# Rows of softmax weights stored token-innermost, denominators per two token tiles, and buffers of one phase handed to the next tile by tile

## The chip, the cores and the metric

The kernel runs on one NeuronCore of one Trainium2 chip. The metric is the device time of one execution in microseconds (us), lower is better; the time given is the median of several runs. A profile is one further execution, recorded instruction by instruction. TensorE is called PE below (PEld: its weight loads), VectorE DVE, ScalarE ACT, GpSimd POOL, and SyncE SP. POOL and SP also issue the DMA transfers, each from a queue that is worked through in order.

## What is computed

The reference is an attention with 32 memory slots, followed by a mixture-of-depths feed-forward step.

```python
# B=8 batches, H=8 heads, S=576 tokens, head_dim=64, 32 memory slots; D=512, F=1024, capacity=128
a = exp(phi - max(phi, axis=2)); a = a / (sum(a, axis=2) + 1e-9)   # softmax over tokens
k_m = einsum('bhsm,bhsd->bhmd', a, k)
v_m = einsum('bhsm,bhsd->bhmd', a, v)
scores = q @ k_m.T / 8;  attn = softmax(scores over the 32 slots)
x = (attn @ v_m), heads side by side                               # (B, S, 512)
score = x @ w_gate
# per batch: the 128 tokens of highest score get x + sigmoid(score) * (relu(x @ w1) @ w2); the others keep x
```

## The kernel before, in words

The program is written in an explicit order: Python generators (`softmax`, `keys`, `split_v`, `values`, `centre`, `scores`, `attend`, `rank`, `gather`, `ffn`) emit instructions and hand over at each `yield`. `turns(jobs, lag, width)` lets several jobs take turns, a new one starting every `lag` rounds; `beside(main, other, n)` gives `other` n steps after each step of `main`. Every engine works through its own instructions in the order in which they were emitted. A tile pool with `bufs` buffers makes a new tile wait for the readers and writers of the tile that had its memory.

There are four phases.

1. Softmax of batches 0 to 3, a group being one batch and four heads (so 8 groups). A group is a tile of 128 partitions (4 heads of 32 slots) by 576 tokens; `softmax` runs its long exact exponential on DVE and ACT and leaves the weights in tile `e` (last instruction L262). Beside it `split_v` (L271 to L279) splits the values into high and low parts and writes them to the DRAM scratch `vparts`.
2. Softmax of batches 4 to 7, and beside it `values(0)`.
3. Attention, ranking and feed-forward of batches 0 to 3, and beside it `values(1)`.
4. The same for batches 4 to 7, with nothing beside it.

After each group's softmax, `keys` (L287 on) turns the weights with six PE transposes (L293) into `aS` with the tokens on the partitions, copies them out with ACT (L295), and after a `yield` splits `aS` on DVE into a high part `ahi` (L299, a mask) and a low part `alo` (L301, a subtraction). POOL then writes both to the DRAM scratch `aparts` in eight DMAs (L305) and doubles them there with two DRAM-to-DRAM copies (L311). The keys' products `k_m` follow on PE (L315).

`values(st)` accumulates `v_m` for four batches exactly from the parts. It loads pieces of 32 tokens (T = 32, 18 pieces): `v_rows` with two DMAs on SP (L334) and `a_rows` with eight DMAs, four on SP and four on POOL (L340), into two buffers each. For each token it issues four matmuls (L353), one per batch, each on 32 rows of the array with a weight load of 128 columns from `a_rows` and 128 moving columns from `v_rows`: 2304 matmuls in each of phases 2 and 3. In `a_rows` the tile is laid out token, head pair, slot, so that the 128 weights of one token lie side by side. A step of the generator is 16 matmuls.

Between phases 2 and 3 the pools of the softmax (`io`, `ex`) are closed, and `work`, `one` and `step` are opened over the same memory. The order on SP there is: the feed-forward weights `w1_sb` (L695) and `w2_sb` (L696), the queries of batch 0 (`load_q`, L100), then the first `v_rows` and `a_rows` of `values(1)`.

`attend` computes for all five token tiles the denominators with ten small matmuls (L493, `heads_of` moving), turns them into reciprocals `rd` on DVE (L498, L500) and a count of good entries (L503), and then goes through the token tiles in pairs: the output products (L510, L512), the scaling by `rd` (L516), POOL's addition of the mean (L519), the score on DVE (L480 to L485) and the store (L523).

Of the kernel before, what the change touches and what calls it, by code (L numbers as in the profile page):

```python
# [18 lines left out]
PSUM = bass.MemoryType.PSUM  # L19

P = 128
NC = 6


# [14 lines left out]
def kernel(  # L39
# [25 lines left out]
    F = w1.shape[1]  # L65
    KD, KF = D // P, F // P
    SET = 4
    T = 32
    scale = 1.0 / Dh ** 0.5
    out_flat = out.rearrange("b s d -> (b s) d")  # L70

# [7 lines left out]
    accp = ctx.enter_context(tc.tile_pool(name="accp", bufs=1, space=PSUM))  # L79
    pss = ctx.enter_context(tc.tile_pool(name="pss", bufs=4, space=PSUM))  # L80
    first = ExitStack()
    io = first.enter_context(tc.tile_pool(name="io", bufs=2))
    ex = first.enter_context(tc.tile_pool(name="ex", bufs=2))

# [27 lines left out]


    v_rows = [rows.tile([P, 2, T, Dh], F32R, name=f"v_rows{i}") for i in range(2)]
    a_rows = [rows.tile([P, T, NPR, M], F32R, name=f"a_rows{i}") for i in range(2)]
    for t in v_rows + a_rows:
        nc.gpsimd.memset(t.bitcast(F32), 0.0)
    for t in kbd + vbd + vls:
# [6 lines left out]
    heads_of = const.tile([P, 4], F32, name="heads_of")  # L125
    ones3 = const.tile([3, P], BF16, name="ones3")
    ones = const.tile([P, 1], F32, name="ones")
    good = const.tile([P, B], F32, name="good")

    tgs = [const.tile([P, NT, 2], F32, name=f"tg{i}") for i in range(3)]  # L130

# [135 lines left out]
    def split_v(b):  # L267

        for u in range(2):
            vb = io.tile([P, S * Dh * NPR // P], F32, name="vb")  # L270
            nc.sync.dma_start(out=vb, in_=v[b, u])  # L271
            hi = io.tile([P, S * Dh * NPR // P], F32, name="vhi")
            nc.vector.tensor_single_scalar(hi.bitcast(I32), vb.bitcast(I32), -4096,
                                           op=ALU.bitwise_and)
            nc.vector.tensor_sub(vb, vb, hi)
            yield
            for vp, src in enumerate((vb, hi)):
                for ap in range(2):
                    nc.gpsimd.dma_start(  # L279
                        out=vparts[u, b, ap, vp].rearrange("r s d -> (r s d)")  # L280
                                                .rearrange("(p x) -> p x", p=P), in_=src)
            yield
# [3 lines left out]
    def keys(b, g):  # L286
        a = soft.pop((b, g))  # L287
        kb = ks.pop((b, g))
        aS = ex.tile([PT, NC, P], F32, name="aS")
        for c0 in range(0, NC, 3):  # L290
            tp = bank([PT, 3, P])
            for c in range(3):
                nc.tensor.transpose(out=tp[:, c], in_=a[:, (c0 + c) * PT:(c0 + c + 1) * PT],  # L293
                                    identity=ident)
            nc.scalar.activation(aS[:, c0:c0 + 3], tp, AF.Copy)  # L295
        yield
        hi = ex.tile([PT, NC, P], F32, name="ahi", bufs=1)
        lo = ex.tile([PT, NC, P], F32, name="alo", bufs=1)
        nc.vector.tensor_single_scalar(hi.bitcast(I32), aS.bitcast(I32), -4096,  # L299
                                       op=ALU.bitwise_and)  # L300
        nc.vector.tensor_sub(lo, aS, hi)  # L301
        for h in range(4):
            r, u = 2 * g + h // 2, h % 2
            for part, src in enumerate((lo, hi)):
                nc.gpsimd.dma_start(  # L305
                    out=aparts[r, u, b, part, 0].rearrange("(c p) m -> p c m", p=PT),
                    in_=src[:, :, h * M:(h + 1) * M])
        for part in range(2):
            copies = aparts[2 * g:2 * g + 2].rearrange("r u b t w s m -> b t w (r u) (s m)")[b, part]
            copies = copies.rearrange("w h (x y) -> w x h y", x=16)  # L310
            nc.gpsimd.dma_start(out=copies[1], in_=copies[0])  # L311
        km = bank([P, 2, 2 * M])
        for rr in range(2):
            for c in range(NC):
                nc.tensor.matmul(out=km[:, rr], lhsT=kb[:, c, rr * P:(rr + 1) * P],  # L315
                                 rhs=aS[:, c, rr * 2 * M:(rr + 1) * 2 * M],
                                 start=(c == 0), stop=(c == NC - 1))
        yield
        for u in range(2):
            part = slice(u * Dh, (u + 1) * Dh)  # L320
            nc.scalar.activation(kbd[b][part, 2 * g:2 * g + 2, u * M:(u + 1) * M],
                                 km[part, :, u * M:(u + 1) * M], AF.Copy)

    def values(st):

        accs = [accp.tile([P, 512], F32, name=f"acc{i}") for i in range(SET)]
        b0 = st * SET

        def load(ch):
            ss = slice(ch * T, (ch + 1) * T)
            for u in range(2):
                nc.sync.dma_start(  # L334
                    out=v_rows[ch % 2][u::2, u].rearrange("p s d -> p (s d)").bitcast(F32),
                    in_=vparts[u, b0:b0 + SET].rearrange("b t w r s d -> (b t w r) (s d)")
                        [:, ch * T * Dh:(ch + 1) * T * Dh])
            for r in range(NPR):
                for u in range(2):
                    (nc.sync, nc.gpsimd)[u].dma_start(  # L340
                        out=a_rows[ch % 2][2 * r + u::8, :, r].bitcast(F32),
                        in_=aparts[r, u, b0:b0 + SET].rearrange("b t w s m -> (b t w) s m")[:, ss])

        n = S // T
        load(0)
        for ch in range(n):
            if ch + 1 < n:
                load(ch + 1)
            vr, ar = v_rows[ch % 2], a_rows[ch % 2]
            for s in range(T):  # L350
                for bb in range(SET):
                    p = slice(bb * 32, bb * 32 + 32)
                    nc.tensor.matmul(out=accs[bb][:, :P].rearrange("p (u d) -> p u d", d=Dh),  # L353
                                     lhsT=ar[p, s].rearrange("p r m -> p (r m)"), rhs=vr[p, :, s],
                                     start=(ch == 0 and s == 0), stop=(ch == n - 1 and s == T - 1))
                if s % 4 == 3:
                    yield
        for bb in range(SET):
            v_m[b0 + bb] = const.tile([P, P], F32, name=f"v_m{b0 + bb}")
            nc.scalar.activation(v_m[b0 + bb], accs[bb][:, :P], AF.Copy)  # L360
# [126 lines left out]
    def attend(b, general):  # L487
        eT, tg = eTs[b % 2], tgs[b % 3]
        row, rest = mean[b]
        den = bank([P, NT, 2, 4])  # L490
        for c in range(NT):
            for g in range(2):
                nc.tensor.matmul(out=den[:, c, g], lhsT=eT[:, g, c * P:(c + 1) * P], rhs=heads_of,  # L493
                                 start=True, stop=True)
        yield
        rd = step.tile([P, NT, H], F32, name="rd")
        rd_f = rd.rearrange("p c h -> p (c h)")
        nc.vector.tensor_scalar(out=rd_f, in0=den.rearrange("p c g h -> p (c g h)"),  # L498
                                scalar1=float(M), scalar2=1e-9, op0=ALU.add, op1=ALU.add)
        nc.vector.reciprocal(rd_f, rd_f)  # L500
        if not general:
            ok = step.tile([P, NT * H], F32, name="ok")
            nc.vector.tensor_scalar(out=ok, in0=rd_f, scalar1=1e-30, scalar2=0.0, op0=ALU.is_gt,  # L503
                                    op1=ALU.add, accum_out=good[:, b:b + 1])
        for c0 in range(0, NT, 2):
            cols = min(2, NT - c0)
            x = step.tile([P, 2, D], F32, name="xj", bufs=3)[:, :cols]
            for c in range(cols):
                o = bank([P, D])
                nc.tensor.matmul(out=o, lhsT=ones3, rhs=rest, start=True, stop=False)  # L510
                for g in range(2):
# [3 lines left out]
                yield  # L515
                nc.vector.tensor_mul(x[:, c].rearrange("p (h d) -> p h d", d=Dh),  # L516
                                     o.rearrange("p (h d) -> p h d", d=Dh),
                                     rd[:, c0 + c].unsqueeze(2).to_broadcast([P, H, Dh]))
            nc.gpsimd.tensor_add(x, x, row.unsqueeze(1).to_broadcast([P, cols, D]))  # L519
            yield  # L520
            score(tg[:, c0:c0 + cols, 1], x, cols)
# [1 line left out]
            nc.gpsimd.dma_start(  # L523
                out=out[b, c0 * P:c0 * P + (cols - 1) * P + n].rearrange("(c p) d -> p c d", p=n),
                in_=x[:n])
        if len(tiles) and tiles[-1] < P:
            nc.gpsimd.memset(tg[tiles[-1]:, NT - 1, 1:2], 0.0)

    def rank(b):
# [102 lines left out]
            in_=ye[:n], in_offset=None)  # L632

    def attention_and_ffn(b, general=False):
        if not general:
            for j in range(2):
                load_q(b, j)
        yield from centre(b)
# [48 lines left out]
    finish(sums)  # L687
    first.close()

    work = ctx.enter_context(tc.tile_pool(name="work", bufs=3))  # L690
    one = ctx.enter_context(tc.tile_pool(name="one", bufs=1))
    step = ctx.enter_context(tc.tile_pool(name="step", bufs=2))
    w1_sb = one.tile([P, KD, F], F32, name="w1_sb")
    w2_sb = one.tile([P, KF, D], F32, name="w2_sb")
    nc.sync.dma_start(out=w1_sb, in_=w1.rearrange("(t p) f -> p t f", p=P))  # L695
    nc.sync.dma_start(out=w2_sb, in_=w2.rearrange("(t p) f -> p t f", p=P))  # L696

# [1 line left out]
    for t in eTs:  # L699
# [4 lines left out]
    finish(sums)  # L704
    finish(turns([attention_and_ffn(b) for b in range(SET, B)], 14, 3))

    ps = bank([1, B])
    nc.tensor.matmul(out=ps, lhsT=ones, rhs=good, start=True, stop=True)
    bad = work.tile([1, B], I32, name="bad")
    nc.vector.tensor_scalar(out=bad, in0=ps, scalar1=-1.0, scalar2=float(P * NT * H),  # L710
                            op0=ALU.mult, op1=ALU.add)
    any_bad = work.tile([1, 1], I32, name="any_bad")
    nc.vector.tensor_reduce(any_bad, bad, axis=AX.X, op=ALU.max)
# [37 lines left out]
```

## Time and profile before

| | |
|---|---|
| Median of 3 runs | 1171.39 us (1164.1 to 1179.52) |
| The profiled execution | 1177.25 us, of which the span of the recorded instructions is 1175.4 us |
| PE busy | 662.3 us, 56% |
| DVE busy | 765.7 us, 65% |
| ACT busy | 293.0 us, 25% |
| POOL busy | 351.3 us, 30% |
| DMA | 165.50 MB in 124930 packets, 84784 of them under 512 B |

The span is the time from the first to the last recorded instruction; the execution's own time is 1.85 us more. Shares of busy time are averages over the four phases, which have different limits, so what follows is read phase by phase. In a row of the timeline the columns are: start, duration, engine, line, operation, output and inputs, number of instructions merged, and in brackets the idle time before with what ended it. A matmul of f32 data that is not marked f32r is recorded as two.

### The profile page before, as it was taken

To read this page: it belongs to the slowest core of one execution; us is meant where nothing else is said; L and a number is where in the kernel's file an instruction comes from. 1 tells how busy PE (TensorE), PEld (TensorE's weight loads), DVE (VectorE), ACT (ScalarE), POOL (GpSimd) and SP (SyncE) were. 2 spreads that over 40 slices of the span, in tenths; PEclk is the share of its full clock that TensorE was granted. 3 is DMA by queue.
4 is the path that set the end of the run, shared out by engine and by line. 5 is a ranking of instruction groups with operands and counts; after the bars stand their busy time and mean duration, and the time that the engine had idled before them with its cause. 6 is when DMAs were issued, how large, how long until landed. Compare 5 with 4: busy or idle time off the path is not lost. (4 is left out here: it accounts for less than half of the span.)

```text
span 1175.4 us, 15823 instructions
## 1 busy us (share of the span) xinstructions
PE 662.3 (56%) x6138; PEld 492.3 (42%) x6138; DVE 765.7 (65%) x1283; ACT 293.0 (25%) x561; POOL 351.3 (30%) x529
## 2 busy tenths in 40 slices
PE   0020202222014777697621259999999977588866
PEld 0020202222014776687621237766766644345432
DVE  8777989999887998999988114343333314565450
ACT  2121312333323332233332010303012121331320
POOL 9133432221124434443212413233232401233230
PEclk9999999999999999999999999999577987598897
DMA  4898994211235979768621656666755712211110
GB/s 139 292 376 296 320 364 130 71 51 26 65 100 108 205 172 226 180 156 156 147 59 40 178 161 159 139 163 142 176 131 128 194 34 66 73 59 38 41 58 13
DMA packets 124930, 165.50 MB, mean 141 GB/s; under 512 B 84784, under 2 KB 95024, under 8 KB 120240
## 3 DMA queue, kind: packets, MB, share of 16 engines
q1 hardware_dynamic: 98352, 84.69, 30.0%
q0 software_dynamic: 26496, 79.72, 21.9%
q8 instruction: 51, 0.84, 0.3%
q14 instruction: 31, 0.25, 0.1%
HBM read 105.64 MB, written 68.16 MB: 148 GB/s over the span
## 5 line engine op out<-in xcount | busy, mean ns | idle before, releaser
L353 PE MATMUL acc<-v_rows,a_rows 32*128 32x128 f32 x4608 | 243.4, 378 | 86.9 <-DMA a_rows<-aparts 86.4
L353 PEld LDWEIGHTS acc<-v_rows,a_rows 32*128 32x128 f32 x4608 | 224.2, 288 | 139.7 <-issue 127.6
L293 PE MATMUL bank<-ident,e 128*96 128x128 f32 x96 | 23.9, 421 | 353.3 <-DVE e L262 353.3
L293 PEld LDWEIGHTS bank<-ident,e 128*96 128x96 f32 x96 | 16.7, 193 | 356.3 <-issue 306.6
L340 POOL DMA_DIRECT2D a_rows<-aparts x144 | 90.2, 633 | 180.2 <-PE acc L353 160.6
L305 POOL DMA_DIRECT2D aparts<-alo x64 | 47.5, 742 | 241.0 <-DVE alo L301 214.7
L315 PE MATMUL bank<-aS,kb 96*128 96x64 f32 x384 | 86.1, 423 | 11.7 <-ACT aS L295 11.7
L315 PEld LDWEIGHTS bank<-aS,kb 96*128 96x128 f32 x384 | 83.1, 331 | 16.6 <-ACT aS L295 15.9
L611 PE MATMUL bank<-w_sb,xeT 128*128 128x512 f32 x128 | 73.0, 709 | 3.4 <-ACT xeT L602 3.4
L519 POOL TENSOR_TENSOR xj<-xj,mean 128x1024 f32<-128x1024 f32 (+1 forms) x24 | 47.7, 1988 | 73.0 <-DVE xj L516 72.9
L512 PE MATMUL bank<-vbd,eT 128*128 128x256 f32 x160 | 66.4, 556 | 0.0
L516 DVE TENSOR_TENSOR xj<-bank,rd 128x512 f32<-128x512 f32 x40 | 27.6, 689 | 56.8 <-PE bank L512 56.6
L622 PE MATMUL bank<-w_sb,hT 128*128 128x512 f32 x128 | 62.3, 620 | 0.2 <-ACT hT L602 0.2
L168 ACT ACTIVATE vh<-num 128x576 int16<-128x576 f32 x32 | 21.8, 682 | 135.3 <-DVE num L212 135.3
L480 DVE TENSOR_TENSOR prod<-xj,wg 128x1024 f32<-128x1024 f32 (+1 forms) x24 | 25.1, 1046 | 46.6 <-POOL xj L519 46.6
L207 DVE SCALAR_TENSOR_TENSOR lo<-num,vh 128x576 f32<-128x576 f32 x48 | 36.2, 754 | 21.7 <-ACT vh L168 21.7
L211 DVE TENSOR_TENSOR low<-low,lo 128x576 f32<-128x576 f32 x64 | 48.5, 758 | 2.2
L305 POOL DMA_DIRECT2D aparts<-ahi x64 | 47.7, 745 | 2.1 <-DMA a_rows<-aparts 1.6
L209 DVE TENSOR_TENSOR lo<-lo,rh 128x576 f32<-128x576 f32 x64 | 48.0, 750 | 0.0
L512 PEld LDWEIGHTS bank<-vbd,eT 128*128 128x128 f32 x160 | 38.4, 265 | 18.7 <-issue 13.7
L556 DVE SCALAR_TENSOR_TENSOR cmp<-row,tg,wide 128x576 bf16<-128x576 f32 x40 | 32.7, 817 | 17.7 <-ACT row L542 16.8
L627 DVE SCALAR_TENSOR_TENSOR ye<-bank,gr,xe 128x512 f32<-128x512 f32 x8 | 6.0, 750 | 56.3 <-PE bank L622 56.3
(152 smaller groups left out, 1269.4 us busy)
## 6 DMA issues: line engine op xcount, KB each, us to landing
v_rows<-vparts SPq DMA_DIRECT2D x72, 512.0 KB, 5.9
vparts<-vb POOLq DMA_DIRECT2D x32, 576.0 KB, 5.9
vparts<-vhi POOLq DMA_DIRECT2D x32, 576.0 KB, 7.7
kb<-in_k SPq DMA_DIRECT2D x16, 576.0 KB, 7.7
vb<-in_v SPq DMA_DIRECT2D x16, 576.0 KB, 7.5
aparts<-aparts POOLq DMA_DIRECT2D x32, 288.0 KB, 3.2
a_rows<-aparts SPq DMA_DIRECT2D x144, 64.0 KB, 6.7
a_rows<-aparts POOLq DMA_DIRECT2D x144, 64.0 KB, 6.1
```

The lines of the kernel that those rows point to most:

```text
L207: stt(out=lo, in0=val, scalar=GRID, in1=h, op0=ALU.mult, op1=ALU.subtract)
L209: tt(out=lo, in0=lo, in1=rh, op=ALU.mult)
L211: tt(out=low, in0=low, in1=lo, op=ALU.add)
L293: nc.tensor.transpose(out=tp[:, c], in_=a[:, (c0 + c) * PT:(c0 + c + 1) * PT], identity=ident)
L305: nc.gpsimd.dma_start(out=aparts[r, u, b, part, 0].rearrange("(c p) m -> p c m", p=PT), in_=src[:, :, h * M:(h + 1) * M])
L315: nc.tensor.matmul(out=km[:, rr], lhsT=kb[:, c, rr * P:(rr + 1) * P], rhs=aS[:, c, rr * 2 * M:(rr + 1) * 2 * M], start=(c == 0), stop=(c = ...
L340: (nc.sync, nc.gpsimd)[u].dma_start(out=a_rows[ch % 2][2 * r + u::8, :, r].bitcast(F32), in_=aparts[r, u, b0:b0 + SET].rearrange("b t w s ...
L353: nc.tensor.matmul(out=accs[bb][:, :P].rearrange("p (u d) -> p u d", d=Dh), lhsT=ar[p, s].rearrange("p r m -> p (r m)"), rhs=vr[p, :, s], ...
L512: nc.tensor.matmul(out=o[:, g * 4 * Dh:(g + 1) * 4 * Dh], lhsT=eT[:, g, (c0 + c) * P:(c0 + c + 1) * P], rhs=vbd[b % 3][:, g], start=False, ...
L519: nc.gpsimd.tensor_add(x, x, row.unsqueeze(1).to_broadcast([P, cols, D]))
L611: nc.tensor.matmul(out=ps[:n], lhsT=xeT[:, d, :n], rhs=w1_sb[:, d, f0:f0 + 512], start=(d == 0), stop=(d == KD - 1))
L622: nc.tensor.matmul(out=ps[:n], lhsT=hT[:, f, :n], rhs=w2_sb[:, f], start=(f == 0), stop=(f == KF - 1))
```

## The change

- `aparts` is laid out in DRAM as 18 pieces of 32 slots by 32 tokens, token innermost. `a_rows` is laid out head pair, slot, token, so a piece's row is 4 KB in one run on both sides, and the weights of one token are read from `a_rows` with a step of 32 elements (128 B).
- The high and low parts are split from `e` itself (128 partitions by 576), ahead of the transposes and of the `yield`, and written to `aparts` from there.
- `vb` and `vhi` of `split_v` get a pool of their own, `vio`. The pools of phases 3 and 4 are opened with `reuse_waits="tile"`, in the order `work`, `weights`, `step`, `one`. The queries of batch 0 are loaded ahead of the feed-forward weights.
- `attend` computes denominators for each pair of token tiles inside the loop, with no `yield` of their own. The count of good entries becomes one comparison on the scores at the end (a score times zero must be zero).

```diff
+    vio = first.enter_context(tc.tile_pool(name="vio", bufs=2))
...
-    a_rows = [rows.tile([P, T, NPR, M], F32R, name=f"a_rows{i}") for i in range(2)]
+    a_rows = [rows.tile([P, NPR, M, T], F32R, name=f"a_rows{i}") for i in range(2)]
...
     def keys(b, g):
         a = soft.pop((b, g))
         kb = ks.pop((b, g))
+        hi = ex.tile([P, S], F32, name="ahi", bufs=1)
+        lo = ex.tile([P, S], F32, name="alo", bufs=1)
+        nc.vector.tensor_single_scalar(hi.bitcast(I32), a.bitcast(I32), -4096, op=ALU.bitwise_and)
+        nc.vector.tensor_sub(lo, a, hi)
+        for h in range(4):
+            r, u = 2 * g + h // 2, h % 2
+            for part, src in enumerate((lo, hi)):
+                nc.gpsimd.dma_start(
+                    out=aparts[r, u, b, part, 0].rearrange("c m s -> m c s"),
+                    in_=src[h * M:(h + 1) * M].rearrange("m (c s) -> m c s", s=T))
+        for part in range(2):
+            copies = aparts[2 * g:2 * g + 2].rearrange("r u b t w c m s -> b t w (r u) (c m s)")[b, part]
+            copies = copies.rearrange("w h (x y) -> w x h y", x=16)
+            nc.gpsimd.dma_start(out=copies[1], in_=copies[0])
         aS = ex.tile([PT, NC, P], F32, name="aS")
...
-        hi = ex.tile([PT, NC, P], F32, name="ahi", bufs=1)
-        lo = ex.tile([PT, NC, P], F32, name="alo", bufs=1)
-        nc.vector.tensor_single_scalar(hi.bitcast(I32), aS.bitcast(I32), -4096,
-                                       op=ALU.bitwise_and)
-        nc.vector.tensor_sub(lo, aS, hi)
...
                 (nc.sync, nc.gpsimd)[u].dma_start(
-                        out=a_rows[ch % 2][2 * r + u::8, :, r].bitcast(F32),
-                        in_=aparts[r, u, b0:b0 + SET].rearrange("b t w s m -> (b t w) s m")[:, ss])
+                        out=a_rows[ch % 2][2 * r + u::8, r].rearrange("p m s -> p (m s)").bitcast(F32),
+                        in_=aparts[r, u, b0:b0 + SET].rearrange("b t w c m s -> (b t w) c (m s)")[:, ch])
...
-                                     lhsT=ar[p, s].rearrange("p r m -> p (r m)"), rhs=vr[p, :, s],
+                                     lhsT=ar[p].rearrange("p r m s -> p (r m) s")[:, :, s], rhs=vr[p, :, s],
...
     def attend(b, general):
-        den = bank([P, NT, 2, 4])
-        for c in range(NT):
-            for g in range(2):
-                nc.tensor.matmul(out=den[:, c, g], lhsT=eT[:, g, c * P:(c + 1) * P], rhs=heads_of,
-                                 start=True, stop=True)
-        yield
-        rd = step.tile([P, NT, H], F32, name="rd")
...
         for c0 in range(0, NT, 2):
             cols = min(2, NT - c0)
+            den = bank([P, 2, 2, 4])[:, :cols]
+            for c in range(cols):
+                for g in range(2):
+                    nc.tensor.matmul(out=den[:, c, g], lhsT=eT[:, g, (c0 + c) * P:(c0 + c + 1) * P],
+                                     rhs=heads_of, start=True, stop=True)
+            rd = step.tile([P, 2, H], F32, name="rd")[:, :cols]
+            nc.vector.tensor_scalar(out=rd.rearrange("p c (g h) -> p c g h", g=2), in0=den,
+                                    scalar1=float(M), scalar2=1e-9, op0=ALU.add, op1=ALU.add)
+            nc.vector.reciprocal(rd, rd)
...
+        if not general:
+            nc.vector.tensor_scalar(out=good[:, b], in0=tg[:, :, 1], scalar1=0.0, scalar2=0.0,
+                                    op0=ALU.mult, op1=ALU.is_equal)
...
-    work = ctx.enter_context(tc.tile_pool(name="work", bufs=3))
-    one = ctx.enter_context(tc.tile_pool(name="one", bufs=1))
-    step = ctx.enter_context(tc.tile_pool(name="step", bufs=2))
-    w1_sb = one.tile([P, KD, F], F32, name="w1_sb")
-    w2_sb = one.tile([P, KF, D], F32, name="w2_sb")
+    work, weights, step, one = (
+        ctx.enter_context(tc.tile_pool(name=name, bufs=bufs, reuse_waits="tile"))
+        for name, bufs in (("work", 3), ("weights", 1), ("step", 2), ("one", 1)))
+    for j in range(2):
+        load_q(0, j)
+    w1_sb = weights.tile([P, KD, F], F32, name="w1_sb")
+    w2_sb = weights.tile([P, KF, D], F32, name="w2_sb")
```

## Prediction

> **What bounds the kernel now.** First the busy time of each engine by phase (columns: stretch in us, its length, then busy us and number of instructions of PE, PEld, DVE, ACT, POOL, then granted clock, DMA share, GB/s).
>
> ```profile
> 0.00:340.00 340.00, 48.12 (x210) 43.68 (x210) 294.38 (x419) 91.36 (x146) 106.75 (x181) 1.00 0.56 192
> 340.00:655.00 315.00, 188.64 (x2574) 180.90 (x2574) 274.76 (x432) 98.11 (x163) 103.48 (x157) 1.00 0.63 137
> 655.00:690.00 35.00, 2.58 (x37) 2.27 (x41) 1.33 (x6) 0.34 (x2) 8.92 (x16) 1.00 0.92 266
> 690.00:950.00 260.00, 255.21 (x2751) 174.92 (x2751) 96.61 (x209) 48.60 (x118) 83.75 (x118) 0.89 0.62 144
> 950.00:1176.00 226.00, 167.72 (x578) 90.51 (x574) 98.62 (x219) 54.56 (x133) 48.38 (x58) 0.80 0.14 46
> ```
>
> Phases 1 and 2 belong to DVE (87% busy in each), phase 3 to PE (98%), phase 4 to PE with gaps. Between 655 and 690 only the DMA engines work (0.92). What each engine waits for, first in phase 2, then on PE in phase 3, says what the gaps are (us in total, times, longest):
>
> ```profile
> DVE lo L207 <- ACT vh L168: 12.0, 16, 0.8
> DVE big L236 <- ACT low L168: 7.6, 9, 0.8
> DVE ahi L299 <- ACT aS L295: 4.4, 2, 2.2
> PE acc L353 <- DMA a_rows<-aparts: 52.6, 8, 14.3
> PE acc L353 <- DMA a_rows<-aparts: 33.8, 2, 32.8
> ```
>
> PE waits 52.6 us for `a_rows` in phase 2, but the phase is DVE's, so they cost nothing. The wait of 32.8 us is the change of phases. The timeline there:
>
> ```profile
> 646.80 0.82 DVE L262 SCALAR_TENSOR_TENSOR e<-e,sm,vh 128x576 f32<-128x576 f32 x1
> 649.19 5.38 PE L315 MATMUL bank<-aS,kb 96*128 96x64 f32 x24
> 649.81 0.56 DVE L299 TENSOR_SCALAR ahi<-aS 96x768 int32<-96x768 int32 x1 [2.19 <-ACT aS L295]
> 650.40 0.95 DVE L301 TENSOR_TENSOR alo<-aS,ahi 96x768 f32<-96x768 f32 x1
> 659.60 0.40 SPq L695 DMA_DIRECT2D w_sb<-in_w  x1
> 660.60 5.38 SPq L100 DMA_DIRECT2D qb<-in_qT  x2
> 675.52 6.78 SPq L340 DMA_DIRECT2D a_rows<-aparts  x4
> 687.42 1.12 PE L353 MATMUL acc<-v_rows,a_rows 32*128 32x128 f32 x16 [32.85 <-DMA a_rows<-aparts]
> 688.88 1.97 PE L353 MATMUL acc<-v_rows,a_rows 32*128 32x128 f32 x32
> ```
>
> SP holds `w1` until 659.60, when everything of the softmax is over; then weights, queries and `v_rows` stand ahead of `a_rows`, and PE starts at 687.42, 39.8 us after `e` was ready (646.80 + 0.82 = 647.62). Last, three rows on the price of a weight load:
>
> ```profile
> 707.85 4.43 PE L493 MATMUL bank<-heads_of,eT 128*128 128x4 f32 x20
> 819.61 0.67 PE L353 MATMUL acc<-v_rows,a_rows 32*128 32x128 f32 x16
> 817.93 1.11 PE L353 MATMUL acc<-v_rows,a_rows 32*128 32x128 f32 x32
> ```
>
> Sixteen more L353 matmuls take 1.97 - 1.12 = 0.85 us at 688, 213 ns for each four, and 0.44 us at 818, 110 ns for each four: TensorE runs at half speed in the first and at full speed in the second. (The clock column shows 1.00 before 783 although the matmuls have the half-speed length; I trust the lengths.) By length 1068 of phase 3's 2304 matmuls are slow and 1236 fast; all of phase 2's are slow. The twenty L493 matmuls have only 4 moving columns and still take 4.43 / 20 = 0.22 us at half speed: a load of 128 columns by itself fills that period. So L353 has no slack in its loads, and a longer load lengthens the period at once.
>
> **The change, part by part.**
>
> *The split (phases 1 and 2).* On 768 columns it takes 0.56 + 0.95 = 1.51 us. On 576 the subtraction is a 128x576 TENSOR_TENSOR, 0.75 us by its row, and the mask 0.56 x 576/768 = 0.42. That saves 0.34 x 16 = 5.4 us of DVE. Phase 1 also waits 19.7 us for `vb` loads, which may swallow part: take 5, bounds 2.5 and 5.4. The split no longer waits for transposes and ACT, so the 4.4 us of `ahi<-aS` go too (bounds 2.2 and 4.4). The new wait of the split, for the previous group's `aparts` writes out of the one `ahi` buffer, was there before and cost nothing: groups are some 19 us apart, eight issues take 5.9 us (0.73 each), and POOL's longest wait ahead of them, for PE to free `a_rows` (L340), is 15.3. If POOL were held up beyond that, DVE would stop, with the other live group's softmax queued behind it, and ACT and PE after that. The writes keep their pieces of 128 B (32 tokens instead of 32 slots) and their number.
>
> *Loads of `a_rows`.* SP's 144 loads are 512 pieces of 128 B each, 73728 of the 84784 small packets; they become 16 pieces of 4 KB. In phase 2 the saving is hidden under DVE, worth nothing. If DVE were not the bound, the 52.6 us of PE's waits would show. In phase 3 PE waits 33.8 - 32.8 = 1.0 us: take 1, bounds 0 and 2.
>
> *The change of phases.* In the built program the first queries wait only for an early reader in the last softmax, so they leave SP some 4 us ahead of `e`'s end and their 1.2 MB are out of the way. `w1` still waits, now for the last L315 that reads a `kb` buffer: 649.19 + 5.38 = 654.6 instead of 659.6. Before, 7.5 MB (weights 4.2, queries 1.2, `v_rows` 1.0, `a_rows` 0.5, copies 0.6) went from 659.6 to 687.4; at the row's 266 GB/s that is 28 us, as seen. After, 6.3 MB from 654.6 take 23.9 us, and I take off 2 for the 128 B pieces, as SP needed 6.78 us for four such issues: start at 676.5, gain 11. Lower bound 5 (only `w1`'s earlier issue). Upper bound 17, if only the chain of `aparts` counted: split 1.2, issues 5.9, wait 2.1, copies 1.1 + 3.2, loads 2.5 + 6.4 = 22.4 after 647.6.
>
> *Denominators.* The 20 recorded matmuls of a batch stay; 12 of them move behind the first pair's products, 0.6 x 2.9 to 4.4 us that no longer stand ahead of the first scaling. In phase 3 PE is full, so nothing changes. In phase 4, where PE is idle 58 of 226 us, this may bring up to 2 us a batch, 8 in all. Against it stand three pairs of small DVE instructions for one (0.20 and 0.40 us now) and a comparison for the count, and three `den` tiles instead of one in the four PSUM banks, which DVE frees; at most 1 us a batch. Phase 3 hides it under PE, phase 4 pays up to 4 if DVE's chain sets the end. One `yield` less brings L353 steps nearer; main still offers more steps than the 144 needed. Take -4, bounds -8 and +4.
>
> *Strided weight loads.* No row of this trace reads an operand of PE with a step, so the price is bounded. Lower end 0: same instruction, size and type. Upper end: a load at half the pace, the price the same load had at half speed (213 against 110 ns) and again the double there. Phase 3 has 1236/4 = 309 fast and 267 slow groups of four: 309 x 0.107 + 267 x 0.213 = 33 + 57 = 90 us. In phase 2, 576 x 0.213 = 123 us more PE raise 188.6 to 312 of 315, and PE would end about 25 us after DVE. So 0 to +115. I take 0, since the nearest row is the load itself, and at half speed an f32 load asks for an element every 213/128 = 1.7 ns, while the 512 bf16 columns of L510 at 713 are through in 0.65 us, 1.3 ns each: PE's reads have some room there. A gain is excluded, since the columns stay 128.
>
> [...]
>
> **Sum.** -5 - 4.4 - 1 - 11 - 4 + 0 = -25.4 us against the profiled execution's 1177.25 (span 1175.4 and 1.85 around it): 1151.9. That execution is 5.9 us over the median of the runs, 1171.39, so the forecast is 1171.39 - 25.4 = 1146. Its own range, with the parts' bounds (-37 to -6 in extremes, seldom all at once) and runs that spread by 15 us: 1130 to 1163.
>
> **The rivals.**
> - *The strided load halves its pace at both speeds.* The place is L353 in phase 3, the price +115, from which the time is 1171.4 - 25.4 + 115 = 1261. It decides against the change from 25.4 / 576 = 44 ns per group of four, 28% on the mean of 156. For it: no slack in the loads. Against: no row shows a stepped read at all.
> - *Only full speed pays.* If memory gives a stepped element each 1.67 ns, the half-speed loads (213 ns for 128) are hardly slowed, the fast ones go from 110 to 213: +33, 1179.
> - *The change of phases gives nothing back*, as the weights still stand ahead of `v_rows` on SP and the late start is a matter of bytes: -5 there instead of -11 and 0 for denominators, 1156.
>
> **How the numbers follow.** Forecast 0.55, loads at half pace or worse 0.25, only full speed 0.12, no gain at the change of phases 0.08. The measurement tells about 2%, 23 us, from no change: faster means under 1148. Of the forecast's 0.55 about 0.37 lie there and 0.18 within 2%; of the 0.20 of the middle cases 0.12 stay within 2% and 0.08 go beyond it to the slow side, since TensorE's fast stretches (the first at 783, with the feed-forward matmuls) may shift by tens of us. With the dear load's 0.25 that makes 0.37, 0.30 and 0.33. The range goes from 1130 to 1265: it takes in the upper end and leaves out loads worse than that and luck below 1130.
>
> **What would show it.** PEld L353 keeps 213 and 110 ns per four; the mask and subtraction come to 1.2 us a group right after L262; SP's packets fall by some 71000; PE's first L353 of phase 3 comes about 29 us after `e`; DVE's wait `ahi<-aS` is gone. Wrong would be: longer L353 periods, PE ending phase 2 after DVE, a first L353 still 35 us or more behind `e`, or new waits of DVE for POOL's DMAs.

## The result, and the profile after

The changed kernel takes 1225.09 us, the median of 4 runs (1215.82 to 1230.48). Beside it the kernel before took 1170.66. The ratio is 1.0452, with a 95% interval of 1.0354 to 1.055: the change makes the kernel about 4.5% slower. Here and below, a run more than 1.5% above the fastest of its kernel counts in the median, but not in ratios, intervals and mean clocks. The profiled execution took 1228.21 us, its span is 1226.0.

The diff has moved the lines a little. `e` now ends at L263, the split is L292 and L293, the writes to `aparts` L297, the copies L303, the parts of the values L274 to L280, the loads of `a_rows` L339, the matmuls of `values` L352, and the feed-forward weights L694 and L695. First the windows by phase of the changed kernel, with the columns as in the prediction; the bounds are the new ends of the phases.

```profile
0.00:340.00 340.00, 48.11 (x210) 43.70 (x210) 290.35 (x408) 89.17 (x142) 101.92 (x181) 1.00 0.56 187
340.00:655.00 315.00, 187.61 (x2547) 180.22 (x2548) 278.55 (x441) 98.74 (x164) 85.37 (x152) 1.00 0.52 144
655.00:685.00 30.00, 7.97 (x54) 7.08 (x51) 1.44 (x4) 1.61 (x5) 10.48 (x20) 1.00 0.89 288
685.00:1023.00 338.00, 331.57 (x2811) 226.35 (x2808) 99.94 (x224) 52.33 (x128) 79.27 (x119) 0.80 0.35 111
1023.00:1226.00 203.00, 152.40 (x527) 83.06 (x525) 100.70 (x231) 51.30 (x124) 50.05 (x57) 0.79 0.16 50
```

Phase 3 is where the time goes. PE is 98% busy in it, but the phase has become 338 us long, with nearly the number of instructions that it had in 287 (both bounds by the last `ye` of the four batches). PEld, which loads the weights, is busy for 226 us. And the granted clock is 0.80. The same view of the kernel before, for its phase 3 by the same bounds (PE is 96% busy by these):

```profile
687.00:974.00 287.00, 276.37 (x2829) 185.72 (x2829) 97.35 (x213) 52.55 (x129) 84.75 (x119) 0.89 0.58 135
```

The change of phases, in the timeline of the changed kernel (columns: start, duration, then what was done, in brackets the idle time before it):

```profile
650.44 1.30 SPq L101 DMA_DIRECT2D qb<-in_qT  x2
...
653.41 0.82 DVE L263 SCALAR_TENSOR_TENSOR e<-e,sm,vh 128x576 f32<-128x576 f32 x1
654.26 0.46 DVE L292 TENSOR_SCALAR ahi<-e 128x576 int32<-128x576 int32 x1
...
654.76 0.76 DVE L293 TENSOR_TENSOR alo<-e,ahi 128x576 f32<-128x576 f32 x1
...
661.21 0.41 SPq L694 DMA_DIRECT2D w_sb<-in_w  x1
...
667.95 7.80 SPq L339 DMA_DIRECT2D a_rows<-aparts  x4
...
683.20 1.15 PE L352 MATMUL acc<-v_rows,a_rows 32*128 32x128 f32 x16 [22.03 <-DMA a_rows<-aparts]
...
684.69 2.03 PE L352 MATMUL acc<-v_rows,a_rows 32*128 32x128 f32 x32
```

`e` ends at 653.41 + 0.82 = 654.23 and PE starts 29.0 us later, against 39.8 before. The queries leave ahead of `e`'s end, the split follows it at once and takes 1.22 us. So this place went as forecast. The last two rows already show the other side: sixteen more matmuls take 2.03 - 1.15 = 0.88 us here at half speed, 220 ns for each four where it was 213. At full speed the same view shows this, where four took 110 ns before:

```profile
819.59 1.10 PE L352 MATMUL acc<-v_rows,a_rows 32*128 32x128 f32 x16
...
825.89 1.99 PE L352 MATMUL acc<-v_rows,a_rows 32*128 32x128 f32 x32
```

1.99 - 1.10 = 0.89 us for sixteen, 222 ns for each four. The matmuls of L352 run at the length of the half-speed clock whichever clock is granted. The recorded part of phase 3 has both: from one start to the next, the median group of four takes 221 ns at recorded full speed and 221 ns at recorded half speed (before: 113 and 214).

A ledger of the two spans, from the last `e` of phases 1 and 2 (the eighth and the sixteenth), the first L352 and the last `ye` (us):

| stretch | before | after | difference |
|---|---|---|---|
| phase 1, to the end of its last `e` | 353.5 | 362.2 | +8.7 |
| phase 2, to the end of its last `e` | 294.1 | 292.0 | -2.1 |
| change of phases, to the first matmul of `values(1)` | 39.8 | 29.0 | -10.8 |
| phase 3, L352 (L353 before) on PE | 106.3 | 143.8 | +37.5 |
| phase 3, the other matmuls on PE | 170.0 | 190.1 | +20.1 |
| phase 3, PE without either | 10.2 | 6.3 | -3.9 |
| phase 4, from the last `ye` of phase 3 | 201.5 | 202.6 | +1.1 |
| span | 1175.4 | 1226.0 | +50.6 |

PE's time is summed from the matmul rows, each one up to its own end or to the start of the next. Three questions follow: is the step of 128 B the cause of the +37.5, what makes the other matmuls slower, and what does phase 1 lose 9 us to?

### The profile page after: what moved, and what is told of

Same layout as the page of the kernel before. It is cut to its first block, busy times and chain, and to the rows that moved or that the text cites. A ratio compares the mean times of both kernels' runs of the same rounds, so it can differ in the third digit from the quotient of the medians.

```text
span 1226.0 us, 15792 instructions
## 1 busy us (share of the span) xinstructions
PE 727.7 (59%) x6138; PEld 540.4 (44%) x6138; DVE 771.0 (63%) x1307; ACT 293.2 (24%) x561; POOL 327.1 (27%) x529
## 5 line engine op out<-in xcount | busy, mean ns | idle before, releaser
L352 PEld LDWEIGHTS acc<-v_rows,a_rows 32*128 32x128 f32 x4608 | 264.7, 308 | 109.7 <-issue 102.3
L352 PE MATMUL acc<-v_rows,a_rows 32*128 32x128 f32 x4608 | 284.8, 417 | 46.9 <-DMA a_rows<-aparts 41.4
L339 POOL DMA_DIRECT2D a_rows<-aparts x144 | 69.6, 490 | 169.8 <-PE acc L352 161.4
L297 POOL DMA_DIRECT2D aparts<-alo x64 | 43.6, 681 | 266.5 <-DVE alo L293 247.0
L608 PE MATMUL bank<-w_sb,xeT 128*128 128x512 f32 x128 | 84.4, 804 | 2.7 <-ACT xeT L599 2.7
L619 PE MATMUL bank<-w_sb,hT 128*128 128x512 f32 x128 | 71.9, 701 | 0.3 <-ACT hT L599 0.3
L440 DVE SCALAR_TENSOR_TENSOR eT<-es,th 128x288 f32<-128x288 f32 x32 | 14.6, 458 | 49.4 <-ACT th L438 49.1
```

What stands on the lines that cost most here:

```text
L297: nc.gpsimd.dma_start(out=aparts[r, u, b, part, 0].rearrange("c m s -> m c s"), in_=src[h * M:(h + 1) * M].rearrange("m (c s) -> m c s", s=T))
L339: (nc.sync, nc.gpsimd)[u].dma_start(out=a_rows[ch % 2][2 * r + u::8, r].rearrange("p m s -> p (m s)").bitcast(F32), in_=aparts[r, u, b0:b0 ...
L608: nc.tensor.matmul(out=ps[:n], lhsT=xeT[:, d, :n], rhs=w1_sb[:, d, f0:f0 + 512], start=(d == 0), stop=(d == KD - 1))
L619: nc.tensor.matmul(out=ps[:n], lhsT=hT[:, f, :n], rhs=w2_sb[:, f], start=(f == 0), stop=(f == KF - 1))
```

## The experiments

The ratios are to runs of the kernel before on the same chip, with 95% intervals. "Step n" means that the 128 weights of a matmul are read n elements of 4 bytes apart. The clock is the mean granted clock over a kernel's runs; that of the kernel before is 0.940 to 0.944, that of the changed kernel 0.914. Kernels that read with another step than their layout asks for mix tokens and slots: the work is the same, the products are other numbers.

| kernel | median us | ratio | mean clock |
|---|---|---|---|
| before, step 2 | 1173.57 (one run) | | 0.942 |
| before, step 4 | 1225.98 (one run) | | 0.933 |
| before, step 32 | 1221.59 | 1.0479 (1.043 to 1.0527) | 0.930 |
| before, step 32 in phase 2 only | 1168.51 | 0.9977 (0.9935 to 1.0018) | 0.944 |
| after, step 1 | 1158.66 | 0.9903 (0.9873 to 0.9934) | 0.946 |
| after, parts of the weights written later | 1219.9 | 1.0368 (1.0301 to 1.0435) | 0.915 |
| before, pools and queries | 1164.45 | 0.9951 (0.9912 to 0.9989) | 0.945 |
| before, denominators in pairs | 1175.0 | 0.9979 (0.9936 to 1.0021) | 0.940 |
| before, pools and denominators | 1162.09 | 0.9912 (0.9864 to 0.996) | 0.941 |
| the same, step 32 | 1228.36 | 1.047 (1.0389 to 1.0551) | 0.906 |
| before, pools and queries, step 32 | 1216.7 | 1.0375 (1.0308 to 1.0443) | 0.928 |
| before, denominators in pairs, step 32 | 1226.51 | 1.048 (1.0382 to 1.0577) | 0.913 |

**The step alone, and the change without it.** Only the operand of the matmul is edited. In the kernel before:

```diff
-  lhsT=ar[p, s].rearrange("p r m -> p (r m)")
+  lhsT=ar[p].rearrange("p t r m -> p (t r m)").rearrange("p (x c k) -> p x c k", c=P, k=32)[:, s // 32, :, s % 32]
```

> The kernel before, with one edit: L353 reads its 128 weights from the same tile with a step of 32 elements (128 B) instead of side by side. The values sums then mix tokens and slots, so v_m and the output are other numbers; the amount of work is the same. Theory 1 (the stepped load is the whole loss of phase 3): groups of four L353 matmuls take about 220 ns at half speed and 205 ns at full speed (before 213 and 110); phase 3 (first L353 to its last ye) grows from 286 us to 335-345, phases 1 and 2 and the change of phases stay (last e at 648, first L353 40 us later): 1215-1230 us. Theory 2 (the loss comes from the order of DMAs and denominators, or from the loads of 4 KB rows): phase 3 stays at 286 us and the time at 1165-1180 us.

And in the changed kernel, the other way round:

```diff
-  lhsT=ar[p].rearrange("p r m s -> p (r m) s")[:, :, s]
+  lhsT=ar[p].rearrange("p r m s -> p (r m s)").rearrange("p (x c) -> p x c", c=P)[:, s]
```

> The changed kernel, with one edit: the 128 weights of a matmul are read side by side instead of with a step of 128 B, everything else as changed. The sums mix tokens and slots, so the output is other numbers. Theory 1: groups of four are back at 213 and 110 ns, phase 3 is back at 286 us, so the time is the changed kernel's 1225 less 54 = 1171; last e stays late at about 654 and the first L353 29 us after it. Theory 2: phase 3 keeps its 340 us and the time stays at 1215-1230 us.

The step alone took 1.0479 of the time before, the whole change 1.0452. The change without it took 0.9903, faster by 8 to 15 us. So the step takes the whole of the loss, and the gain of the rest with it. The step costs more in the changed kernel (1225.09 against 1158.66, 66 us) than by itself (51 us), so the 1171 that were expected without it were 12 us too many; a later experiment looks for the difference. In the profile of the step alone, at full speed:

```profile
789.08 1.11 PE L353 MATMUL acc<-v_rows,a_rows 32*128 32x128 f32 x16
791.40 1.99 PE L353 MATMUL acc<-v_rows,a_rows 32*128 32x128 f32 x32
```

That is (1.99 - 1.11) / 4 = 220 ns for each four, as in the changed kernel, and L353 takes 142.1 us of PE in phase 3 (106.3 before). Of the 576 groups of four, those that had full speed doubled; the others hardly changed. The expectation had 205 ns at full speed; it is the same 220 as at half speed.

**Which step pays.** The same edit with k = 4 (16 B from one weight to the next) and with k = 2 (8 B).

> As step32, with a step of 4 elements (16 B); output other numbers for the same reason. [...]

> [...]

Step 4 took 1225.98 us, step 2 took 1173.57, one run each beside 1170.3 and 1171.34 of before. The timelines at full speed, of step 4 and then of step 2:

```profile
808.91 1.16 PE L353 MATMUL acc<-v_rows,a_rows 32*128 32x128 f32 x16
810.58 2.09 PE L353 MATMUL acc<-v_rows,a_rows 32*128 32x128 f32 x32
```

```profile
790.13 1.16 PE L353 MATMUL acc<-v_rows,a_rows 32*128 32x128 f32 x32
...
794.60 0.69 PE L353 MATMUL acc<-v_rows,a_rows 32*128 32x128 f32 x16
```

Step 4: (2.09 - 1.16) / 4 = 233 ns for each four. Step 2: (1.16 - 0.69) / 4 = 118 ns, where before has 110. At full speed twice the distance is nearly free here, four times costs the whole price (233 ns, above the 220 of the step of 32), thirty-two times no more. A price that grew with the distance is out: it sets in between 8 B and 16 B from one weight to the next. What makes it there was not shown.

**Whether half speed is free of it.** The step of 32 for the products of phase 2 alone, which runs at half speed throughout:

```diff
-  lhsT=ar[p, s].rearrange("p r m -> p (r m)")
+  lhsT=ar[p].rearrange("p t r m -> p (t r m)").rearrange("p (x c k) -> p x c k", c=P, k=32)[:, s // 32, :, s % 32] if st == 0 else ar[p, s].rearrange("p r m -> p (r m)")
```

> The kernel before, with the step of 128 B in phase 2's matmuls alone (phase 3 reads side by side); half of the v_m are other numbers. Theory: the stepped load takes 220 ns per four at half speed, where the plain one takes 213, phase 2 runs at half speed throughout and belongs to DVE, so nothing is lost: 1165-1178 us, last e at 648. Rival (a stepped load costs in either phase, since it holds up the transposes behind it and DVE after them): last e 655 or later, 1180 us or more.

The ratio is 0.9977 (0.9935 to 1.0018). The windows of this kernel show why phase 2 does not care:

```profile
340.00:655.00 315.00, 193.27 (x2574) 185.66 (x2574) 274.18 (x432) 98.47 (x163) 104.55 (x159) 1.00 0.64 137
```

PE is busy for 193.3 us, 4.6 more than before's 188.6, while DVE has 274.2 of 315. At half speed the step costs 7 ns for each four (220 against 213), and DVE's work covers that.

**The pools and the first queries.** In the kernel before, `vio`, `reuse_waits="tile"` and the queries ahead of the weights, and nothing else of the change:

```diff
+    vio = first.enter_context(tc.tile_pool(name="vio", bufs=2))
...
+    work, weights, step, one = (
+        ctx.enter_context(tc.tile_pool(name=name, bufs=bufs, reuse_waits="tile"))
+        for name, bufs in (("work", 3), ("weights", 1), ("step", 2), ("one", 1)))
+    for j in range(2):
+        load_q(0, j)
```

> The kernel before, with only the pools' part of the change: vio for vb and vhi, reuse_waits by tile, the first queries ahead of the feed-forward weights. Theory 1: phases 1 to 2 end as before (last e at 648), the first L353 comes 29-32 us after e instead of 40, phases 3 and 4 as before: 1160-1164 us. Rival (the gain at the change of phases came from the early split and the 4 KB rows, not from the pools): first L353 38-40 us after e, 1168-1173 us.

The ratio is 0.9951 (0.9912 to 0.9989), some 6 us less. In its timeline:

```profile
643.05 4.43 SPq L101 DMA_DIRECT2D qb<-in_qT  x2
...
646.01 0.82 DVE L263 SCALAR_TENSOR_TENSOR e<-e,sm,vh 128x576 f32<-128x576 f32 x1
...
677.11 1.12 PE L354 MATMUL acc<-v_rows,a_rows 32*128 32x128 f32 x16 [23.32 <-DMA a_rows<-aparts]
```

PE starts 677.11 - 646.83 = 30.3 us after `e`, where the changed kernel has 29.0 and the kernel before 39.8. So 9.5 of the 10.8 us come from handing the memory on tile by tile and from the order of the loads, which were not tried apart, and 1.3 are left for the early split and the longer pieces.

**What phase 1 lost.** The first four `e` end at 68.8, 126.5, 176.6 and 212.4 us before and at 68.5, 128.6, 186.7 and 222.2 in the changed kernel: 2 us are lost between the first and the second, 8 between the second and the third, and nothing after that. Of the waits of DVE in the first 340 us (total us, times, longest) those for the parts of the values, first before, then after:

```profile
DVE vhi L273 <- DMA vb<-in_v: 19.7, 5, 5.5
```

```profile
DVE vhi L274 <- DMA vb<-in_v: 21.5, 4, 12.3
...
DVE vhi L274 <- DMA aparts<-ahi: 4.2, 1, 4.2
```

A new wait of 12.3 us for `vb`, and one that the profile puts down to the writes of `ahi`. The timeline of the changed kernel between its second and third `e` shows the place of the first:

```profile
130.67 1.36 DVE L276 TENSOR_TENSOR vb<-vb,vhi 128x1152 f32<-128x1152 f32 x1
...
133.49 0.70 POOL L297 DMA_DIRECT2D aparts<-alo  x1 [4.90 <-DVE alo L293]
...
140.93 1.10 POOL L303 DMA_DIRECT2D aparts<-aparts  x2 [1.92 <-DMA aparts<-ahi]
142.02 0.55 POOL L280 DMA_DIRECT2D vparts<-vb  x1
...
147.93 7.94 SPq L272 DMA_DIRECT2D vb<-in_v  x2
...
156.73 0.76 DVE L274 TENSOR_SCALAR vhi<-vb 128x1152 int32<-128x1152 int32 x1 [12.35 <-DMA vb<-in_v]
```

DVE has the low part of the values ready at 130.67 + 1.36 = 132.0, but POOL first issues the eight writes of `aparts`, waits for them to land, issues the two copies, and writes `vparts` at 142.02, 10 us late. Its buffer comes free later, so the next load of `vb` leaves SP at 147.93, and DVE waits for it with the softmax queued behind. Around the first `e` it is the same: a low part ready at 79.1 is written at 89.31 (80.26 before). In the kernel before:

```profile
130.19 1.06 POOL L279 DMA_DIRECT2D vparts<-vb  x2 [3.73 <-DVE vb L275]
...
148.85 1.10 POOL L279 DMA_DIRECT2D vparts<-vb  x2
...
163.28 0.76 DVE L273 TENSOR_SCALAR vhi<-vb 128x1152 int32<-128x1152 int32 x1 [2.77 <-DMA vb<-in_v]
```

There the write left at 130.19, as soon as DVE was done. The ten DMAs of `aparts` came after it and held up the next write, ready at 138.2, to 148.85, just as long; but by then DVE had another part of the values and more of the softmax to work on, and waited only 2.8 us. So what costs in these rows is not that ten DMAs stand ahead of a write of `vparts`, but which write they stand ahead of. To show this, the changed kernel with only the writes and the copies emitted where they stood before, after the transposes and the `yield`; the split itself stays early and from `e` (the step of 32 is kept):

```diff
         nc.vector.tensor_single_scalar(hi.bitcast(I32), a.bitcast(I32), -4096, op=ALU.bitwise_and)
         nc.vector.tensor_sub(lo, a, hi)
+        aS = ex.tile([PT, NC, P], F32, name="aS")
+        for c0 in range(0, NC, 3):
...
+            nc.scalar.activation(aS[:, c0:c0 + 3], tp, AF.Copy)
+        yield
         for h in range(4):
...
             nc.gpsimd.dma_start(out=copies[1], in_=copies[0])
-        aS = ex.tile([PT, NC, P], F32, name="aS")
-        for c0 in range(0, NC, 3):
...
-            nc.scalar.activation(aS[:, c0:c0 + 3], tp, AF.Copy)
-        yield
```

> The changed kernel, stepped weight loads and all, with one edit: the writes and copies of aparts are emitted after the yield, where they stood before, while the split itself stays early. Theory: phase 1 lost 10 us because the early writes and copies went ahead of the vparts writes in POOL's queue, where the copies wait for the writes to land; then the fourth e is back at 211-214 us (changed 222), the last at 644-648 (changed 654), and the time 1213-1219 us (changed 1225). Rival (the shape of the writes, 32 partitions instead of 96, or the place of vb and vhi in memory costs the 10 us): fourth e at 220-223, 1222-1228 us.

It took 1219.9 us, 1.0368 (1.0301 to 1.0435) of the time before, a little above the 1213 to 1219 that were expected. The fourth `e` ends at 209.2 us (222.2 in the changed kernel, 212.4 before), phase 1 at 349.1 (362.2 and 353.5), phase 2 at 641.1 (654.2 and 647.6). Its waits of DVE in the first 340 us:

```profile
DVE vhi L274 <- DMA vb<-in_v: 10.1, 4, 4.2
...
DVE vhi L274 <- DMA aparts<-alo: 2.7, 1, 2.7
```

The wait of 12.3 is gone. With the writes and copies in this place the early split gains 6.5 us over both phases; with them in the place of the change it loses 6.6. The medians differ by only 5.2 us, 1219.9 against 1225.09, and the two intervals overlap, so the 13 us rest on the profiles: in the eleven kernels that keep the split of before, the last `e` ends between 645.7 and 649.8 us, in the two with the split of the change at 654.2 and 654.4 (the changed kernel, and the one that reads it side by side).

**The denominators.** In pairs, with the comparison for the count, in the kernel before:

```diff
-        den = bank([P, NT, 2, 4])
...
-        yield
-        rd = step.tile([P, NT, H], F32, name="rd")
...
         for c0 in range(0, NT, 2):
             cols = min(2, NT - c0)
+            den = bank([P, 2, 2, 4])[:, :cols]
...
+            rd = step.tile([P, 2, H], F32, name="rd")[:, :cols]
```

> The kernel before with the denominators per two token tiles alone. Forecast theory: they bring up to 4 us (ratio 0.996-0.999). If the shorter phases 3 of the kernels with them (275 and 280 us against 287) are theirs: 1159-1164 us, ratio about 0.992. If those were scatter of the clock: 1168-1173 us.

And with the pools, the same plus the edit of the pools above:

> The kernel before, with the pools' part and the denominators per two token tiles, nothing else. If denominators in pairs gain, phase 3 goes from 287 to about 280 us (as the kernel with weights side by side had it) and the time from 1164 to 1154-1159; if they do nothing, 1161-1167; if their extra DVE work or banks cost, 1168 or more.

The denominators alone give 0.9979 (0.9936 to 1.0021), between a gain of 7.5 us and a loss of 2.5. With the pools it is 0.9912 (0.9864 to 0.996), whose interval overlaps that of the pools alone. What they bring is too small for these runs. The kernel with both keeps the weights side by side and is about 1% faster than the kernel before, let alone the changed one; the one with the pools alone is about 0.5% faster.

**Where the gain of the pools goes beside the step.** Both of these edits and the step of 32:

> The kernel before with the pools' part, the denominators per two tiles, and the step of 128 B in the weight loads; the split and the layout in DRAM stay as before, and the output is other numbers as in step32. Without the step it took 1162 us. If the step costs the same whatever stands around it, phase 3 takes 320-332 us (275 without the step, plus the 45 that step32 showed) and the time is 1205-1213 us. If denominators in pairs and the step together let TensorE's clock fall more often, as the changed kernel's phase 3 of 340-343 us suggests, phase 3 takes 337-345 us, with full speed in 110-118 us of it instead of 136, and the time is 1215-1225 us.

1228.36 us: with the stepped loads the two edits no longer gain anything over the step alone (1221.59), and the time is above both ranges that were expected. To find which of them is to blame, each alone beside the step:

> The kernel before with the denominators per two token tiles and the weights of L353 read with a step of 32 elements (so the products use other weights); pools, order of loads and split as before. Open is why the stepped load costs 58 us together with the new pools and the denominators (1228 against 1170.5 for both, read side by side: pools and denominators alone gave -10), though the same load cost 53 alone. If denominators in pairs give PE a denser mix beside the stepped loads and the granted clock falls: about 1231 to 1234, granted clock about 0.91, other matmuls of phase 3 near 193 us. If the shorter pause at the change of phases lowers the clock: like the step alone, 1222, clock 0.93, other matmuls near 183 us.

> The kernel before with the pools and loads of the change (own pool for the parts of the values, memory handed on tile by tile, first queries ahead of the weights) and the weights of L353 read with a step of 32 elements (so the products use other weights); denominators and split as before. If the denominators are what lowers the granted clock beside stepped loads: 1222 less the 6 that the pools gave alone, so about 1216 at a clock of 0.93. If the shorter pause at the change of phases lowers it: about 1228 at 0.91. If it is neither alone, both kernels lie near 1222 and the interaction stays open.

By the medians the pools keep their gain (1216.7 against 1221.59), the denominators do not (1226.51, between the two times that were expected), though the intervals overlap. The clock separates them. All 8 runs with the step of 32 and whole denominators have a mean granted clock of 0.925 to 0.930. All 16 runs with the step and denominators in pairs (the changed kernel and the one that writes later among them) have 0.901 to 0.922. Without the step the denominators don't show in the clock: 0.940 in both kernels of that comparison. Phase 3 in the windows, of the step alone and then of the step with the denominators:

```profile
686.00:1018.00 332.00, 325.11 (x2829) 227.98 (x2829) 97.59 (x213) 52.51 (x128) 84.76 (x119) 0.85 0.50 116
```

```profile
685.00:1021.00 336.00, 329.50 (x2829) 225.44 (x2829) 100.45 (x224) 52.51 (x128) 88.23 (x119) 0.82 0.49 115
```

The same 2829 matmuls, the same step, and a clock of 0.82 instead of 0.85, from 0.89 in the kernel before. (The record of the clock begins at 770 to 783 us; what lies before counts as full speed in all of these means, although the lengths of the matmuls say half. So a part of the distance between 0.82 and 0.85 is only that the one record begins at 770 us and the other at 783: at recorded full speed are 131 us of the one phase and 136 of the other.) The other matmuls of phase 3 take 183.1 us with the step alone, 183.3 with the pools, 186.2 with the denominators and 192.4 with both, against 170.0 before. So of the +20.1 us of the ledger, 13.1 come with the step by itself, and the other 7 lie between the 3.1 and the 9.1 us that the denominators add beside the step (186.2 - 183.1, 192.4 - 183.3). That it is the clock which lengthens them can be reckoned: with each kind of matmul at the mean length that it has at full and at half speed in phase 3 of the seven kernels that read side by side or with a step of 2 there, and the unrecorded stretch taken as half speed, they come to 182.8 us for the step alone and 189.7 for the changed kernel (measured 183.1 and 190.1). What the clock responds to was not found. And the price of the denominators beside the step, 5 us in one comparison and 12 in the other, is not settled, since the intervals of the times overlap.

## Why the prediction was wrong, point by point

The prediction forecast 1146 us and faster; the time was 1225.09. That lies in the range of 1130 to 1265, but only because the range was stretched to a dear load, to which 0.25 was given; the sum's own range ended at 1163. One term failed, and with it the sign.

- **Strided weight loads (forecast 0, measured +37.5 in L352 and, with the clock, some 13 more): the step that failed.** The choice of the lower end rested on "the nearest row is the load itself" and on the 1.3 ns per column at which L510 read bf16. Neither row reads with a step, so neither said anything about a stepped one; they bounded what a read in one run can do. What the runs showed in its place: with 128 B between the weights one came through every 1.7 ns at either clock (220/128), with 16 B every 1.8 ns at full speed (233/128). That takes the four loads of a group as running at once: after the change each is recorded with a median of 310 ns, while its group takes 221. The condition for the sign, 44 ns per group of four on the mean, was right: the step added 37.5 us / 576 = 65 ns.
- **The rivals.** "Only full speed pays" named what came, 213 ns for the fast groups (measured 221) and nearly nothing for the slow ones (221 against 214), and its +33 us are close to the +37.5. Its time of 1179 was still 46 us short. It left out that the other matmuls slow down with the clock (+20), it counted 25 us of gains, of which the split's 9 became a loss of 7 and the denominators' 4 did not show. "Half pace at both speeds" came nearer in time (1261) and is wrong on half speed: phase 2 shows 220 against 213 ns, and no cost. "The change of phases gives nothing back" falls with the 29.0 us.
- **The split (forecast -5 and -4.4, measured +6.6 over phases 1 and 2).** Its size lay within the bounds, its place wasn't followed through every queue. Mask and subtraction took 0.46 + 0.76 us (forecast 0.42 + 0.75), the wait of `ahi` for ACT's `aS` is gone, and with the writes in the later place the two terms came to -6.5. The prediction looked at POOL's queue for phase 2 and for the one `ahi` buffer. It didn't ask what the eight writes and the two waiting copies are now ahead of in phase 1: the writes of `vparts`, and with them DVE's next `vb`. Its 19 us from group to group are wrong as well: the ends of `e` lie 34 to 58 us apart before.
- **Loads of `a_rows` (forecast -1).** The page of the changed kernel has

```profile
DMA packets 53506, 165.50 MB, mean 135 GB/s; under 512 B 11056, under 2 KB 21296, under 8 KB 48816
```

  71424 packets fewer, as forecast, and PE's waits for `a_rows` in phase 2 fell from 52.6 to 19.4 us, worth nothing there, as forecast.
- **The change of phases (forecast -11, measured -10.8).** Right, and by its reason: the pools alone gave 9.5 of it.
- **Denominators (forecast -4, bounds -8 and +4).** Alone, the interval of -7.5 to +2.5 us allows it and does not show it. Beside the stepped loads the effect has the other sign in the medians, and the mean clock is 0.901 to 0.922 instead of 0.925 to 0.930, which no row of before could have told.

Of the five signs named, four came: the packets, the start 29 us after `e`, the lost wait, and the 1.2 us for the split. The first in the list, the lengths of 213 and 110 ns, did not, and it decided. Two of the signs of a wrong forecast were seen: longer L352 periods, and the new wait of DVE, for a load held back by POOL's queue.

## What to carry to other kernels

A layout that makes a transfer's rows longer can be paid for by whoever reads the tile: here the rows of 4 KB came with a step of 128 B in the reads, and the full-speed group of four matmuls went from 113 to 221 ns. Where PE's weight loads set the pace, time the stepped read alone first (a step of 2 f32 took 118 ns here against 110 side by side, a step of 4 took 233; 3 was not tried), or look for the transfer's gain elsewhere. Where a price can't be read from any row, the point from which it turns the sign (here 44 ns for four matmuls) tells whether it may be taken as nothing; a step no row shows, under the engine that is 98% busy, may not. And an instruction that moves up is ahead of everything that its queue held between (here a write of `vparts`, 10 us late), in every phase, not only in the one that is looked at.

## What was not expected of the hardware

- The stepped f32 weight loads did not follow the clock: with 128 B between the weights four matmuls with loads of 128 columns took 220 ns at half and at full speed, against 213 and 110 ns side by side.
- The step of 16 B was dearer than that of 128 B: 233 against 220 ns for each four at full speed, and L353 took 149.7 us of PE in phase 3 against 142.1.
- The granted clock switched between half and full while PE was 96 to 98% busy, and not equally in kernels with the same number of matmuls: 0.89, 0.85, 0.82 and 0.80 in phase 3 (before, the step, the step with denominators in pairs, the whole change). In the recorded part of phase 3, full speed was granted for 126 of 191 us before and for 112 of 249 after.
